# Where the queries of batch 0 are scaled, and which engine copies its first x out of PSUM, in a fused retention and feed-forward kernel

## The chip, the cores and the metric

The kernel runs on one core of one Trainium2 chip. The metric is the device time of an execution in microseconds (us): lower is better. A core has TensorE (PE, with its weight loads listed as PEld), VectorE (DVE), ScalarE (ACT), GpSimd (POOL) and SyncE (SP), which here only issues DMAs. Each engine works through its own queue in order and waits on semaphores for the others.

## The reference

Retention over 8 batches, 8 heads, 576 positions and a head dimension of 64 gives x; a feed-forward layer with a tanh gelu follows. Inputs and output are 32-bit floats, PE works in 16 bits.

```python
scale = 1.0 / np.sqrt(D_)                       # D_ = 64
scores = scale * np.matmul(q, k.transpose(0, 1, 3, 2))
gamma = 1.0 - 2.0 ** (-5.0 - np.arange(H))      # one decay per head
Dmat = np.where(rel >= 0, gamma[:, None, None] ** rel[None, :, :], 0.0)   # rel = i - j
attn = np.matmul(scores * Dmat[None], v)
x = attn.transpose(0, 2, 1, 3).reshape(B * S, H * D)                      # 4608 x 512
g = gelu_tanh(x @ w_in)                          # 512 x 2048
out = g @ w_out                                  # 2048 x 512
```

## The kernel before

**Attention of one batch.** The decay gamma^(i-j) is split into a factor of the query's position and a factor of the key's. The key's factor is put on the values when they are cast (`cast_v`, L260, values times `sc`). The query's factor, with the scale, is put on x when it leaves PSUM (`evac`, L593, times the table `gx`). Between positions i >= j inside a chunk only a mask is then left (`mask_sc`, L451: scores `st` times `cm` into `ret`).

576 positions are four chunks of 128 and a tail of 64. Two chunks are a *half* `s` (0 or 1), four heads a group `hh` (0 or 1). For each of the four (s, hh): `load_qkv` brings 256 KB of k, q or v; `cast_qk` casts k and q to 16 bits through `copy` (L247) on an engine that the plan names; `tr` (L361) transposes them on PE, and copies the result `tr` to `T` (L247); `back` (L421) transposes the keys back and copies them to `kq`; `score_mm` (L438) makes the scores `st`. For each half, `state_mm` (L506) makes the chunks' states `us` from keys and values, `scan` (L522 adds into `vs`, L526 multiplies by `gt` into `ws`) carries the state from chunk to chunk, `put` casts it into the block-diagonal buffer `tbd` (two casts of 64 partitions; with `S2` one goes to ACT and one to DVE), `values` (L553) multiplies `ret` with the values into `xs`, `inter_mm` (L580) adds the part of the earlier chunks from `tbd`, and `evac` writes x. `tbd` has two buffers, for even and odd batches, zeroed by `tbd_zero` with four memsets each (L133); `inter_tail` does the same as `evac` for the tail.

Batch 0 loads its keys and queries in a layout of its own (`R4`: four positions per partition, two heads), so that one load serves a pair of heads of both halves. A transposed pair is copied by two instructions.

**Feed-forward.** `Block.up` (L641, tile `hp`) and `up_half` (L727) multiply x with `w_in_sb` and ACT applies the gelu into `gT`; `mix_sa`, `mix_sc` and `mix_d` form sums and differences of `gT` on DVE or GpSimd for a fast product scheme; `product` (L783) multiplies them with `w_out_sb`, and `settle` adds the results up. `cast_w_in(j, i, engine)` casts a quarter of a row block of w_in. A block needs x of a whole pair of batches or of a half; the first call, `F0.up_half(0, 1)`, needs two evacuated blocks of batch 0 and w_in(0, 0 to 3).

**The order** is written out by hand. `run(units, plan)` calls units of the feed-forward in turn (units 0 to 9 are empty, 10 and 11 are the first two up_half), and after each unit the steps that the plan lists for it, in the order in which they are listed. The order of those calls is the order of each engine's queue. The letters name the engine: G is GpSimd, V is DVE, A is ACT, S2 halves between ACT and DVE.

```python
    def run(units, plan):
        for i, f in enumerate(units):
            f()
            for step in plan.get(i, ()):
                step()
```

Loads go out on SP's queue in the order in which they are written; each waits for a free buffer. `warm` (L139) and `pad` (L150) put dummy matmuls on zeros in front of PE's work, so many 128-column pieces as the table `pads` gives for a place.

Of the kernel before, what the change touches and what calls it, by code (L numbers as in the profile page):

```python
# [10 lines left out]
AF = mybir.ActivationFunctionType  # L11
ALU = mybir.AluOpType
# [7 lines left out]
def kernel(  # L20
# [53 lines left out]
    for hf in half:  # L74
        nc.gpsimd.iota(p2[hf, 0:2], pattern=[[1, 2]], base=-64, channel_multiplier=2,
                       allow_small_or_imprecise_dtypes=True)
        nc.gpsimd.iota(p2[hf, 2:3], pattern=[[0, 1]], base=-64, channel_multiplier=1,
                       allow_small_or_imprecise_dtypes=True)
    ident = const.tile([128, 128], F16, name="ident")
# [18 lines left out]
    sc = const.tile([128, 2 * H + 4], F32, name="sc")  # L98
    for hh in range(2):
        nc.vector.tensor_tensor(  # L100
            out=ex[:, 8 * hh : 8 * hh + 8].rearrange("p (r h) -> p r h", r=2),
            in0=p2[:, 0:2].unsqueeze(2).to_broadcast([128, 2, 4]),
            in1=lg[:, 4 * hh : 4 * hh + 4].unsqueeze(1).to_broadcast([128, 2, 4]),
            op=ALU.mult,
        )
# [7 lines left out]

    def mask():
        c = cm.rearrange("p r s i -> p (r s i)")
        nc.vector.tensor_tensor(out=c, in0=c, in1=p2[:, 0:1].to_broadcast([128, 256]), op=ALU.is_ge)


    gx = const.tile([128, HP, 2, 64], F32, name="gx")
    for p in range(HP):  # L120
        nc.scalar.activation(out=gx[:, p], in_=gi, func=AF.Exp, bias=lg[:, 12:13], scale=lg[:, 8 + p : 9 + p])
    nc.scalar.activation(out=sc, in_=ex, func=AF.Exp, bias=0.0, scale=-1.0)
    gt = const.tile([128, HP], F32, name="gt")
# [3 lines left out]

    R4 = {(0, "k"), (0, "q")}
# [120 lines left out]
    def cast_qk(b, s, hh, key, eng):  # L249
        t = att[b].pop((key, s, hh))  # L250
        o = att[b]["kq"][:, s, hh, "kq".index(key), :]
        if (b, key) in R4:
            copy(eng, o.rearrange("p (r h d) -> p r h d", r=4, h=2), t.rearrange("p (h r d) -> p r h d", r=4, h=2))
        else:
            copy(eng, unperm(o), perm(t))
        done(t)
# [14 lines left out]
    def cast_tail(b, key, eng):  # L271
        a = att[b]
        t = a.pop((key, "t"))
        if key != "v":
            copy(eng, a["kqt"][:, "kq".index(key), :], t[:, 0:256])
            done(t)
            return
        eng.tensor_tensor(
            out=a["vt"].rearrange("p (h d) -> p h d", d=D),
            in0=t[:, 0:256].rearrange("p (h d) -> p h d", d=D),  # L280
            in1=sc[:, 16:20].unsqueeze(2).to_broadcast([128, 4, D]),
            op=ALU.mult,
        )
        done(t)
# [307 lines left out]
    def evac(b, s, c):  # L592
        nc.vector.tensor_tensor(  # L593
            out=xb[b][:, :, 2 * s + c].rearrange("p s q i -> p q s i"),
            in0=att[b]["x", s][c].rearrange("p (q s i) -> p q s i", q=4, s=2),
            in1=gx,
            op=ALU.mult,
        )

    def inter_tail(b):  # L600
        a = att[b]
        xs = a.pop("xt")
        for u in range(2):
            for s in range(2):
# [6 lines left out]
            nc.vector.tensor_tensor(  # L611
                out=xt[:, :, b, 2 * u : 2 * u + 2, :].rearrange("p s q i -> p q s i"),
                in0=xs[u][:, 0:128].rearrange("p (q i s) -> p q s i", q=2, s=2),
                in1=gx[:, 2 * u : 2 * u + 2, :, 0:32],
                op=ALU.mult,
            )
# [274 lines left out]
    def add(plan, *entries):  # L891
# [13 lines left out]
    load_qkv(0, 1, 0, "k", None)  # L905
    load_qkv(0, 1, 0, "q", None)
    load_qkv(0, 0, 1, "k", None)
# [6 lines left out]
    load_qkv(0, 1, 0, "v", None)  # L914
    load_qkv(0, 1, 1, "v", None)
    load_w_in(0, 0, E)
# [5 lines left out]
    load_w_in(1, 0, E2)  # L922
    load_w_in(2, 2, None)
    load_qkv(1, 0, 0, "k", None)
# [24 lines left out]
    load_w_out(5, E3)  # L949
    load_w_out(7, E3)  # L950
# [3 lines left out]
    load_w_out(11, H)  # L954
# [5 lines left out]
    load_qkv(2, 1, 0, "k", None)  # L960
    load_qkv(2, 0, 0, "q", None)
    load_qkv(2, 0, 0, "k", None)
    load_qkv(2, 0, 1, "q", None)
    load_qkv(2, 1, 0, "q", None)
    load_qkv(2, 0, 0, "v", None)
    load_qkv(3, 0, 1, "k", None)
    load_qkv(2, 0, 1, "k", None)
    load_qkv(2, 0, 1, "v", None)
    load_qkv(2, 1, 1, "k", None)
    load_qkv(2, 1, 1, "v", None)  # L970
    load_qkv(3, 0, 0, "q", None)
# [3 lines left out]
    load_qkv(3, 0, 0, "k", None)  # L975
    load_qkv(3, 0, 1, "q", None)
    load_qkv(3, 0, 1, "v", None)
    load_tail(1)
    load_qkv(3, 1, 1, "k", None)
# [9 lines left out]
        ("tr", 0, 1, 0, 0): 7,  # L989
        ("tr", 0, 1, 1, 0): 0,  # L990
# [6 lines left out]
        ("bk", 0, 1, 1): 1,  # L997
        ("us", 0, 0): 2,
# [5 lines left out]
        ("tr", 0, 0, 0, 1): 9,  # L1004
# [5 lines left out]
        ("tr", 0, 1, 0, 1): 1,  # L1010
        ("in", 0, 1): 11,
# [8 lines left out]
    def turn():  # L1020
# [8 lines left out]
        (0, L(cast_qk, 0, 0, 0, "q", A)),  # L1029
        (1, L(new_x, 0)),  # L1030
        (0, L(cast_qk, 0, 0, 0, "k", V)),
        (0, L(tr, 0, 0, 0, 0, V)),
        (0, L(cast_qk, 0, 1, 0, "k", A)),
        (0, L(cast_qk, 0, 1, 0, "q", V)),
        (0, L(mask)),
        (0, L(tr, 0, 0, 0, 1, V)),
        (0, L(tr, 0, 1, 0, 0, V)),
        (2, L(score_mm, 0, 0, 0)),
        (2, L(mask_sc, 0, 0, 0)),
        (2, L(score_mm, 0, 1, 0)),  # L1040
        (2, L(back, 0, 0, 0, V)),
        (1, L(tr, 0, 1, 0, 1, S2)),
        (0, L(cast_qk, 0, 0, 1, "k", A)),
        (3, L(tr, 0, 1, 1, 1, S2)),
        (1, L(cast_qk, 0, 0, 1, "q", G)),
        (2, L(back, 0, 1, 0, A)),
        (0, L(tr, 0, 0, 1, 0, S2)),
        (1, L(cast_qk, 0, 1, 1, "q", G)),
        (5, L(back, 0, 0, 1, A)),
        (3, L(tr, 0, 0, 1, 1, A)),  # L1050
        (1, L(cast_qk, 0, 1, 1, "k", G)),
        (3, L(tr, 0, 1, 1, 0, A)),
        (5, L(mask_sc, 0, 0, 1)),
        (3, L(mask_sc, 0, 1, 0)),
        (5, L(state_mm, 0, [0])),
        (4, L(score_mm, 0, 0, 1)),
        (4, L(cast_v, 0, 0, 0, G)),
        (5, L(scan, 0, 0)),
        (5, L(values, 0, 0)),
        (6, L(score_mm, 0, 1, 1)),  # L1060
        (6, L(put, 0, 0, A)),
        (3, L(cast_v, 0, 0, 1, G)),
        (5, L(scan, 0, 1)),
        (1, L(inter_mm, 0, 0, 0)),
        (5, L(put, 0, 1, S2)),
        (7, L(back, 0, 1, 1, A)),
        (6, L(mask_sc, 0, 1, 1)),
        (8, L(inter_mm, 0, 0, 1)),
        (5, L(evac, 0, 0, 0)),
        (8, L(evac, 0, 0, 1)),  # L1070
        (9, L(inter_mm, 0, 1, 0)),
        (6, L(cast_v, 0, 1, 1, G)),
        (7, L(state_mm, 0, [1])),
        (5, L(cast_v, 0, 1, 0, G)),
        (7, L(scan, 0, 2)),
        (7, L(put, 0, 2, S2)),
        (8, L(inter_mm, 0, 1, 1)),
        (9, L(evac, 0, 1, 0)),
        (7, L(values, 0, 1)),
        (9, L(cast_w_in, 0, 2, G)),  # L1080
        (0, L(tbd_zero, 0, G)),
        (7, L(tbd_zero, 1, G)),
        (11, L(scan, 0, 3)),
        (9, L(evac, 0, 1, 1)),
        (7, L(cast_w_in, 0, 3, A)),
# [4 lines left out]
        (11, L(put, 0, 3, V)),  # L1090
        (12, L(cast_qk, 1, 0, 0, "k", G)),
        (14, L(cast_w_in, 2, 3, G)),
        (11, L(cast_qk, 1, 0, 1, "k", V)),
        (7, L(cast_w_in, 1, 3, A)),
        (10, L(cast_w_in, 2, 1, A)),
        (12, L(F0.mix_sc, 0, 2, V)),
        (8, L(cast_w_in, 1, 1, A)),
        (7, L(cast_w_in, 1, 0, V)),
        (10, L(cast_w_in, 2, 2, V)),
        (12, L(F0.mix_sa, 0, 2, V)),  # L1100
        (9, L(cast_w_in, 2, 0, V)),
        (18, L(F0.mix_d, 0, 2, V)),
        (7, L(turn)),
        (7, L(cast_w_in, 1, 2, A)),
        (19, L(F0.mix_sc, 2, 2, V)),
        (10, L(cast_qk, 1, 0, 0, "q", A)),
        (18, L(cast_qk, 1, 0, 1, "q", V)),
        (19, L(cast_w_in, 3, 0, A)),
        (19, L(tr, 1, 0, 1, 1, A)),
        (15, L(tr, 1, 0, 1, 0, S2)),  # L1110
        (15, L(tr, 1, 0, 0, 0, S2)),
        (17, L(cast_w_in, 3, 2, G)),
        (19, L(score_mm, 1, 0, 0)),
        (19, L(F0.mix_sa, 2, 2, G)),
        (22, L(mask_sc, 1, 0, 1)),
        (27, L(scan, 1, 1)),
        (29, L(inter_mm, 1, 0, 0)),
        (15, L(tr, 1, 0, 0, 1, S2)),
        (21, L(cast_v, 1, 0, 1, V)),
        (19, L(cast_w_in, 3, 1, A)),  # L1120
        (20, L(cast_v, 1, 0, 0, G)),
        (21, L(F0.mix_d, 2, 2, V)),
        (20, L(mask_sc, 1, 0, 0)),
        (21, L(new_x, 1)),
        (22, L(state_mm, 1, [0])),
        (24, L(cast_qk, 1, 1, 0, "k", G)),
        (21, L(score_mm, 1, 0, 1)),
        (14, L(cast_w_in, 3, 3, G)),
        (22, L(scan, 1, 0)),
        (22, L(put, 1, 0, A)),  # L1130
        (23, L(inter_mm, 1, 0, 1)),
        (20, L(cast_qk, 1, 1, 0, "q", A)),
        (22, L(values, 1, 0)),
        (29, L(put, 1, 1, A)),
        (27, L(F0.mix_sc, 4, 2, G)),
        (23, L(cast_qk, 1, 1, 1, "q", A)),
        (25, L(cast_v, 1, 1, 0, V)),
        (25, L(tr, 1, 1, 0, 0, V)),
        (23, L(evac, 1, 0, 1)),
        (21, L(cast_qk, 1, 1, 1, "k", A)),  # L1140
        (22, L(evac, 1, 0, 0)),
        (22, L(F0.mix_sa, 4, 2, G)),
        (27, L(cast_v, 1, 1, 1, V)),
        (24, L(tr, 1, 1, 0, 1, A)),
        (28, L(state_mm, 1, [1])),
        (28, L(F0.mix_d, 4, 2, V)),
        (27, L(tr, 1, 1, 1, 0, A)),
        (31, L(mask_sc, 1, 1, 0)),
        (28, L(score_mm, 1, 1, 0)),
        (29, L(score_mm, 1, 1, 1)),  # L1150
        (27, L(tr, 1, 1, 1, 1, A)),
        (31, L(mask_sc, 1, 1, 1)),
        (32, L(inter_mm, 1, 1, 1)),
        (29, L(scan, 1, 2)),
        (29, L(put, 1, 2, A)),
        (30, L(mix_w_out, 0, "sums", G)),
# [3 lines left out]
        (31, L(inter_mm, 1, 1, 0)),  # L1160
        (32, L(mix_w_out, 1, "sums", G)),
        (28, L(mix_w_out, 1, "copy", A)),
# [83 lines left out]
        (48, L(inter_tail, 0)),  # L1246
# [317 lines left out]
```

## Time and profile before

| | before |
|---|---|
| median of 4 runs | 298.24 us (298.08 to 298.73) |
| the profiled execution | 298.08 us, of which the span is 296.3 |
| PE busy | 290.1 us (98% of the span) |
| DVE busy | 238.6 us (81%) |
| ACT busy | 164.0 us (55%) |
| POOL busy | 98.2 us (33%) |
| first feed-forward matmul (L727) | at 22.63 us |

Times in the profile count from the start of the span. "Busy" adds up the execution of instructions on an engine, whatever they wait for elsewhere; a busy PE includes dummy matmuls. In a view with `<-` in brackets, the number is the idle time ahead of an instruction and the name is what ended it. A group's row gives the operation, output <- input with partitions x elements and type, how many there were, their busy time and the mean time of one in ns.

### The profile page before, as it was taken

What the parts mean: (1) busy time and instruction counts of PE and PEld (TensorE: products, weight loads), DVE (VectorE), ACT (ScalarE), POOL (GpSimd) and SP (SyncE); (2) the same over time, 40 slices, a digit from 0 to 9 for tenths busy, and PEclk for the clock granted to TensorE, in tenths of its full rate; (3) what the DMA queues carried; (4) which work ended last, traced back from release to release, by engine and by line L of the source; (5) the groups of instructions that cost most, each with busy time, mean ns of one, the idle gap of its engine ahead of it and who ended that gap; (6) DMA issues with size and microseconds to landing.
All of it is one profiled execution on the core that took longest, in us unless ns stands there. A gap on an engine that the chain in (4) does not pass through costs nothing.

```text
span 296.3 us, 8812 instructions
## 1 busy us (share of the span) xinstructions
PE 290.1 (98%) x3689; PEld 207.0 (70%) x3689; DVE 238.6 (81%) x456; ACT 164.0 (55%) x320; POOL 98.2 (33%) x131
## 2 busy tenths in 40 slices
PE   8989999999999999999999999999999999999995
PEld 5657478888885568655875587558754886787684
DVE  3898889989997999888569846899688198886773
ACT  7449889973736672565446544554445316605830
POOL 4572595056260336075037006698000000000000
PEclk9999999999999999999999999999999999999999
DMA  6999999767799989995996989482120002002204
GB/s 206 337 341 318 312 382 320 208 167 209 194 254 221 254 254 162 271 317 107 203 300 214 160 216 280 129 152 12 52 92 2 1 28 117 2 0 73 71 0 144
DMA packets 92663, 52.48 MB, mean 177 GB/s; under 512 B 38352, under 2 KB 86480, under 8 KB 92624
## 3 DMA queue, kind: packets, MB, share of 16 engines
q1 hardware_dynamic: 92288, 51.26, 64.4%
q10 hardware_dynamic: 336, 0.66, 0.8%
q8 instruction: 29, 0.48, 0.7%
q14 instruction: 10, 0.08, 0.1%
HBM read 36.70 MB, written 9.44 MB: 156 GB/s over the span
## 4 chain that ended last, share of the span: by engine, by line
PE 92%; ACT 4%; DVE 2%; issue 1%; DVEq 0%; ACTq 0%
PE hp L641 30%; PE my L783 11%; PE mz L783 10%; PE hp L727 6%; PE mu L783 5%; PE mv L783 5%; PE mw L783 5%; PE xs L553 3%; PE st L438 3%; PE py L671 2%; PE xs L580 2%; PE us L506 2%; PE tr L361 1%; PE warm L139 1%; PE pv L671 1%; PE tr L150 1%
## 5 line engine op out<-in xcount | busy, mean ns | idle before, releaser
L641 PE MATMUL hp<-x,w_in_sb 128*128 128x512 f16 x400 | 92.4, 379 | 0.5 <-ACT gT L645 0.2
L645 ACT ACTIVATE gT<-hp 128x512 f16<-128x512 f32 x108 | 63.8, 597 | 44.2 <-PE hp L641 43.5
L641 PEld LDWEIGHTS <-w_in_sb 128*128 128x128 f16 x432 | 40.8, 98 | 43.0 <-issue 0.7
L783 PEld LDWEIGHTS <-gT 128*128 128x128 f16 x576 | 55.8, 98 | 8.1 <-ACT gT L714 0.2
L451 DVE TENSOR_TENSOR ret<-st,cm 128x512 f16<-128x512 f32 x64 | 40.0, 680 | 4.2 <-PE st L438 4.2
L260 POOL TENSOR_TENSOR cv<-ld,sc 128x512 f16<-128x512 f32 x28 | 30.2, 1095 | 34.5 <-DMA ld<-in_v_dram 34.5
L247 POOL CAST kq<-ld 128x512 f16<-128x512 f32 x27 | 18.8, 702 | 56.5 <-DMA ld<-in_k_dram 33.9
L247 ACT CAST tbd<-ws 64x256 f16<-64x256 f32 x56 | 22.3, 402 | 22.1 <-DVE ws L526 21.6
L783 PE MATMUL my<-w_out_sb,gT 128*128 128x256 f16 x288 | 34.5, 273 | 0.0
L783 PE MATMUL mz<-w_out_sb,gT 128*128 128x256 f16 x288 | 34.4, 273 | 0.0
L783 PEld LDWEIGHTS <-gsum 128*128 128x128 f16 x288 | 28.0, 98 | 3.3
L752 DVE TENSOR_TENSOR gsum<-gT 128x1024 f16<-128x1024 f16 x35 | 28.0, 801 | 1.4 <-ACT gT L733 0.8
L756 DVE TENSOR_TENSOR gT<-gT 128x1024 f16<-128x1024 f16 x35 | 28.8, 841 | 0.2
L593 DVE TENSOR_TENSOR x<-xs,gx 128x512 f16<-128x512 f32 x32 | 21.7, 683 | 3.9 <-PE xs L580 3.7
L744 DVE TENSOR_TENSOR gdia<-gT 128x512 f16<-128x512 f16 (+1 forms) x32 | 17.0, 532 | 5.0 <-ACT gT L645 2.6
L810 DVE TENSOR_TENSOR ost<-ost,mv 128x512 f32<-128x512 f32 x18 | 11.5, 681 | 11.6 <-issue 7.5
L247 ACT CAST kq<-ld 128x512 f16<-128x512 f32 x27 | 16.4, 616 | 4.8 <-DMA ld<-in_q_dram 3.1
L727 PE MATMUL hp<-x,w_in_sb 128*128 128x256 f16 x160 | 18.8, 273 | 0.0
L783 PE MATMUL mw<-w_out_sb,gdia 128*128 128x256 f16 x144 | 17.2, 273 | 0.0
L783 PE MATMUL mu<-w_out_sb,gsum 128*128 128x256 f16 x144 | 17.2, 273 | 0.0
L783 PE MATMUL mv<-w_out_sb,gsum 128*128 128x256 f16 x144 | 17.2, 273 | 0.0
L727 PEld LDWEIGHTS <-w_in_sb 128*128 128x128 f16 x160 | 15.3, 98 | 2.2 <-issue 0.3
(119 smaller groups left out, 396.6 us busy)
## 6 DMA issues: line engine op xcount, KB each, us to landing
ld<-in_k_dram SPq DMA_DIRECT2D x30, 256.0 KB, 5.0
ld<-in_q_dram SPq DMA_DIRECT2D x30, 256.0 KB, 5.5
ld<-in_v_dram SPq DMA_DIRECT2D x30, 256.0 KB, 5.6
out_dram<-ost SPq DMA_DIRECT2D x14, 512.0 KB, 5.4
loan<-in_moe_w_out_dram SPq DMA_DIRECT2D x12, 256.0 KB, 5.8
loan<-in_moe_w_in_dram SPq DMA_DIRECT2D x8, 256.0 KB, 6.8
ld<-in_moe_w_in_dram SPq DMA_DIRECT2D x8, 256.0 KB, 5.8
ld<-in_moe_w_out_dram SPq DMA_DIRECT2D x4, 256.0 KB, 5.4
```

The lines of the kernel that those rows point to most:

```text
L247: (eng.copy if eng is nc.scalar else eng.tensor_copy)(out=out, in_=in_)
L260: eng.tensor_tensor(out=unperm(att[b]["v"][:, s, hh, :]), in0=perm(t), in1=sc[:, 8 * hh : 8 * hh + 8] .rearrange("p (r h) -> p r h", r=2) ...
L451: nc.vector.tensor_tensor(out=x.rearrange("p (a m) -> p a m", a=2), in0=st[hl].rearrange("p (a m) -> p a m", a=2), in1=cm.rearrange("p r s ...
L593: nc.vector.tensor_tensor(out=xb[b][:, :, 2 * s + c].rearrange("p s q i -> p q s i"), in0=att[b]["x", s][c].rearrange("p (q s i) -> p q s ...
L641: nc.tensor.matmul(hp, w_in_sb[:, ct, 128 * f : 128 * f + 128], x[:, :, ct, :], start=(ct == 0), stop=(ct == 3),)
L645: nc.scalar.activation(out=self.g(f // 2)[:, f % 2], in_=hp, func=AF.Gelu_apprx_tanh)
L727: nc.tensor.matmul(hp[:, 256 * h : 256 * h + 256], w_in_sb[:, ct, 256 * j + 128 * h : 256 * j + 128 * h + 128], xb[self.b][:, :, 2 * u : 2 ...
L744: e.tensor_tensor(out=self.sa[:, j : j + n], in0=g[:, :, 0, 0:256], in1=g[:, :, 1, 256:512], op=ALU.add)
L752: e.tensor_tensor(out=self.sc[:, j : j + n], in0=g[:, :, 0], in1=g[:, :, 1], op=ALU.add)
L756: e.tensor_tensor(out=g.rearrange("p j h c -> p j (h c)")[:, :, 256:768].rearrange("p j (h c) -> p j h c", h=2), in0=g[:, :, :, 0:256], in ...
L783: nc.tensor.matmul(t[u] if isinstance(t, list) else t[:, 256 * u : 256 * u + 256], lhs(j, slice(128 * u, 128 * u + 128)), w_out_sb[:, j, w ...
L810: nc.vector.tensor_tensor(out=out, in0=in0, in1=t, op=op)
```

## The change

**Queries of batch 0 are scaled at their cast** (`QS = {0}`). Two new tables hold the query's factor: `sq4` for batch 0's layout (from four new IOTAs `p4`, a product on DVE and an exp on ACT that is placed ahead of the four of `gx`) and `sq` for the tail (an exp on ACT after that of `sc`). Casting a query becomes a product with a table, and goes to DVE or GpSimd instead of ACT, DVE or GpSimd. **The four `evac` of batch 0 become copies on ACT**, where they were products on DVE; the tail's two become copies on DVE.

**Steps change place and engine.** In batch 0: the first k cast goes from DVE to GpSimd, the copy of its transpose from DVE to ACT, the last k cast (0,1,1) from GpSimd to DVE, the copy of back(0,0,0) from DVE to ACT; `tbd_zero(1)` now follows the GpSimd cast of w_in(0,2) instead of leading it. Later: the casts of w_in(1,3) and (1,1) go from ACT to GpSimd and w_in(1,2) from ACT to DVE; cast_v(1,1,0) from DVE to GpSimd; the copies of tr(1,1,0,0) from DVE to ACT and of tr(1,0,0,0) from both to DVE; put(1,1) from ACT to both. Some loads and some dummy matmuls move.

```diff
+    p4 = const.tile([128, 4], F32, name="p4")
+    for i in range(4):
+        nc.gpsimd.iota(p4[32 * i : 32 * i + 32], pattern=[[1, 4]], base=-64, channel_multiplier=4,
+                       allow_small_or_imprecise_dtypes=True)
...
+    sq4 = const.tile([128, 4, H], F32, name="sq4")
+    nc.vector.tensor_tensor(
+        out=sq4,
+        in0=p4.unsqueeze(2).to_broadcast([128, 4, H]),
+        in1=lg[:, 0:H].unsqueeze(1).to_broadcast([128, 4, H]),
+        op=ALU.mult,
+    )
...
     gx = const.tile([128, HP, 2, 64], F32, name="gx")
+    nc.scalar.activation(out=sq4, in_=sq4, func=AF.Exp, bias=lg[:, 12:13], scale=1.0)
     for p in range(HP):
         nc.scalar.activation(out=gx[:, p], in_=gi, func=AF.Exp, bias=lg[:, 12:13], scale=lg[:, 8 + p : 9 + p])
     nc.scalar.activation(out=sc, in_=ex, func=AF.Exp, bias=0.0, scale=-1.0)
+    nc.scalar.activation(out=sq, in_=ex, func=AF.Exp, bias=lg[:, 12:13], scale=1.0)
...
         if (b, key) in R4:
-            copy(eng, o.rearrange("p (r h d) -> p r h d", r=4, h=2), t.rearrange("p (h r d) -> p r h d", r=4, h=2))
+            o = o.rearrange("p (r h d) -> p r h d", r=4, h=2)
+            i = t.rearrange("p (h r d) -> p r h d", r=4, h=2)
+            if key == "q" and b in QS:
+                g = 2 * (2 * hh + s)
+                f = sq4[:, :, g : g + 2].unsqueeze(3).to_broadcast([128, 4, 2, D])
+                eng.tensor_tensor(out=o, in0=i, in1=f, op=ALU.mult)
+            else:
+                copy(eng, o, i)
...
-    def evac(b, s, c):
+    def evac(b, s, c, eng=None):
+        if b in QS:
+            copy(
+                eng,
+                xb[b][:, :, 2 * s + c].rearrange("p s q i -> p q s i"),
+                att[b]["x", s][c].rearrange("p (q s i) -> p q s i", q=4, s=2),
+            )
+            return
...
     load_qkv(0, 1, 0, "k", None)
+    load_qkv(0, 0, 1, "k", None)
     load_qkv(0, 1, 0, "q", None)
-    load_qkv(0, 0, 1, "k", None)
...
     load_qkv(0, 1, 0, "v", None)
+    load_w_in(0, 0, E)
     load_qkv(0, 1, 1, "v", None)
-    load_w_in(0, 0, E)
...
-        ("tr", 0, 1, 0, 0): 7,
-        ("tr", 0, 1, 1, 0): 0,
+        ("tr", 0, 1, 0, 0): 5,
+        ("tr", 0, 1, 1, 0): 4,
...
-        (0, L(cast_qk, 0, 0, 0, "q", A)),
+        (0, L(cast_qk, 0, 0, 0, "q", V)),
         (1, L(new_x, 0)),
-        (0, L(cast_qk, 0, 0, 0, "k", V)),
-        (0, L(tr, 0, 0, 0, 0, V)),
+        (0, L(cast_qk, 0, 0, 0, "k", G)),
+        (0, L(tr, 0, 0, 0, 0, A)),
...
-        (2, L(back, 0, 0, 0, V)),
+        (2, L(back, 0, 0, 0, A)),
...
+        (2, L(cast_qk, 0, 1, 1, "k", V)),
         (1, L(cast_qk, 0, 1, 1, "q", G)),
...
-        (1, L(cast_qk, 0, 1, 1, "k", G)),
...
+        (5, L(evac, 0, 0, 0, A)),
+        (7, L(inter_mm, 0, 0, 1)),
         (6, L(mask_sc, 0, 1, 1)),
-        (8, L(inter_mm, 0, 0, 1)),
-        (5, L(evac, 0, 0, 0)),
-        (8, L(evac, 0, 0, 1)),
+        (8, L(evac, 0, 0, 1, A)),
...
+        (7, L(cast_w_in, 0, 2, G)),
         (7, L(values, 0, 1)),
-        (9, L(cast_w_in, 0, 2, G)),
+        (9, L(evac, 0, 1, 0, A)),
+        (7, L(tbd_zero, 1, G)),
         (0, L(tbd_zero, 0, G)),
-        (7, L(tbd_zero, 1, G)),
+        (9, L(evac, 0, 1, 1, A)),
         (11, L(scan, 0, 3)),
-        (9, L(evac, 0, 1, 1)),
...
-        (7, L(cast_w_in, 1, 3, A)),
+        (9, L(cast_w_in, 1, 3, G)),
...
-        (8, L(cast_w_in, 1, 1, A)),
+        (8, L(cast_w_in, 1, 1, G)),
...
-        (7, L(cast_w_in, 1, 2, A)),
+        (8, L(cast_w_in, 1, 2, V)),
...
-        (25, L(cast_v, 1, 1, 0, V)),
-        (25, L(tr, 1, 1, 0, 0, V)),
+        (25, L(tr, 1, 1, 0, 0, A)),
+        (25, L(cast_v, 1, 1, 0, G)),
...
-        (48, L(inter_tail, 0)),
+        (48, L(inter_tail, 0, V)),
```

Of `pads`, five more places change by one or two pieces: tr(0,0,0,1) from 9 to 11, us(0,0) from 2 to 3, in(0,1) from 11 to 10, bk(0,1,1) and tr(0,1,0,1) from 1 to 0. In all two pieces of 128 columns more are multiplied, in one instruction fewer. In the loads, k(1,0,0) moves one place ahead, w_out(11) four ahead, and those of batches 2 and 3 change places among themselves by up to seven.

## The prediction

> **What bounds the kernel now.** I read the slices first, then what PE waits for, then the chain of waits where PE does wait, then the timeline of the other engines there. The page's slices (each 7.4 us):
>
> ```profile
> PE   8989999999999999999999999999999999999995
> DVE  3898889989997999888569846899688198886773
> PEclk9999999999999999999999999999999999999999
> ```
>
> TensorE works at its full clock all through; only the first three slices leave room. The view of what PE waits for between 0 and 22.6 us has four rows, two of which can be moved by this change:
>
> ```profile
> PE us L506 <- ACT kq L247: 0.6, 1, 0.6
> PE xs L553 <- DVE ret L451: 0.2, 1, 0.2
> ```
>
> (line <- what it waited for: us in all, times, longest.) The same view from 22.6 to 110 us shows one row of 0.2 us. So the 273.7 us from the first feed-forward matmul (hp L727, at 22.63) to the end of the span are matmul work, and **the time moves with the moment at which hp L727 starts**. Much of PE's work ahead of it is dummy matmuls (L139, L150), so a busy PE hides real waits there. The chain of waits shows them:
>
> ```profile
> 17.16 1.19 DVE tbd L247
> 18.35 0.03 issue
> 18.38 0.69 DVE x L593
> 19.07 1.21 DVE ret L451 x2
> 20.27 0.04 issue
> 20.32 0.41 PE xs L553 x15
> 20.73 0.70 PE us L150 x3
> ...
> 22.63 3.65 PE hp L727 x32
> ```
>
> (start, length, what.) For 3 us VectorE is the chain: half a put, an evacuation, two masked scores. Beside the chain, on DVE, stand the last scan and put of batch 0, and around them, on the timeline:
>
> ```profile
> 20.18 0.41 DVE L522 TENSOR_TENSOR vs<-us,ws 128x256 f32<-128x256 f32 x1
> 20.70 0.43 DVE L526 TENSOR_TENSOR ws<-vs,gt 128x256 f32<-128x256 f32 x1
> 21.23 0.29 DVE L247 CAST tbd<-ws 64x256 f16<-64x256 f32 x1
> 16.29 1.92 POOL L133 MEMSET tbd<- 128x512 f16 x4
> 18.30 0.59 ACT L247 COPY kq<-tr 128x512 f16<-128x512 f16 x1
> 18.93 0.32 PE L506 MATMUL us<-cv,kq 64*64 64x64 f16 x16 [0.59 <-ACT kq L247]
> 12.30 4.04 POOL L260 TENSOR_TENSOR cv<-ld,sc 128x512 f16<-128x512 f32 x4 [0.68 <-DMA ld<-in_v_dram]
> ```
>
> The same half put takes 0.29 at 21.23 and 1.19 at 17.16, and ends just after GpSimd's four memsets of the second tbd buffer: 0.90 us are a blocked DVE.
>
> **What the Trainium skill says.** "SBUF — State Buffer", section "Who interferes with whom": a DVE copy or cast in a two-port mode and a GpSimd instruction lock each other out for a whole instruction; a DVE operation with two SBUF inputs is disturbed by GpSimd reads, not by one that only writes. The trace agrees on both: the cast above (1.19 against 0.29), and a two-input scan at 16.63, under the same memsets, took its usual 0.42. "TensorE: Matmul & The Clock Gate", section "What's actually happening": the clock halves after an idle window of about 3.4 us; here the longest wait ahead of hp was 1.1 us and the clock stayed whole, so a wait that grows by tenths costs its length only.
>
> **The change, part by part.** Prices, from the groups by shape:
>
> ```profile
> L260 DVE TENSOR_TENSOR cv<-ld,sc 128x512 f16<-128x512 f32 x2 | 1.4, 691 | 0.0
> L817 ACT COPY ost<-mw 128x512 f32<-128x512 f32 x9 | 5.3, 586 | 6.0 <-PE mw L783 6.0
> L260 POOL TENSOR_TENSOR cv<-ld,sc 128x512 f16<-128x512 f32 x28 | 30.2, 1095 | 34.5 <-DMA ld<-in_v_dram 34.5
> ```
>
> (busy us, mean ns.) They stand for a scaled query cast on DVE (0.69, in place of a cast of 0.43), an evacuation as a ScalarE copy (0.59, in place of 0.68 on DVE) and a scaled query cast on GpSimd (1.10, 1.04 where it ran alone, in place of 0.61).
>
> *Set-up.* Four IOTAs on GpSimd (0.13 each, those of p2), one small DVE product (about 0.16, as ex), two more exps on ACT (0.2 busy, step 0.11, as sc and gt). sq4 is the first of ACT's exps and waits for GpSimd's four IOTAs, so gx, sc, gt, the table load and the first ACT job slip by some 0.5 us (5.39 to 5.9). Queued behind them is now the copy of the first transposed keys, which DVE started at 6.07: level to 0.1 late.
>
> *Up to 15.65.* The second half's keys load one place earlier and the first half's second query one later. Successive loads were first used at 7.42, 8.10 and 8.91, so a place is 0.7 to 0.8 us: k01, cast on ACT at 8.10, lands about 7.4; q10, cast on DVE at 7.42, lands 8.1 and costs 0.69 instead of 0.43. Both feed transposes ahead of which dummy matmuls stand: two pieces of 128 columns fewer before one, two and four more before two others; with the smaller changes two more in all, at some 0.06 us each (the chain's twelve at 20.73 took 0.70). The copy of back(0,0,0) moves from DVE to ACT, which stood idle for 2.02 us before 11.91. k11 moves from GpSimd (its second cast at 10.46 to 11.63) to DVE; q11 takes its time there as a product, so the four value casts still start when v lands (12.30). All of it ends in the scan at 15.65, with a chain of matching length: 0, between −0.3 and +0.3.
>
> *15.65 to hp.* tbd_zero(1) now comes behind the cast of w_in(0,2), whose load keeps its place (17.29), so the put at 17.16 finds GpSimd idle: −0.90. The evacuation L593 at 18.38 leaves DVE (step 0.61). The two masked scores then run from 17.75 to 19.03, not 18.99 to 20.27; their scores were complete at 17.71. ACT does the other half puts (17.15 to 17.55), then the first evacuation (0.6), w_in(0,3) (0.6) and only then the kq copy: 18.5 to 19.1 instead of 18.30 to 18.88. PE's second half of us waits for that copy and ends at 19.47, not 19.25. This is **what is late next**: the last scan, which started at 20.18 because DVE was busy, starts at 19.5 because PE delivers then. Scan 19.5 to 20.45, put (halves on ACT and DVE) to 20.9, then PE's last inter steps, which took 0.97 from 21.66 to 22.63: hp at 21.95, **−0.7**. The values need the masked scores at 19.03, so their 0.2 us goes too, inside this gap.
>
> *Can hp be ready?* It needs two evacuated x blocks and w_in(0,3), (0,2), (0,1), (0,0). On GpSimd: (0,2) 17.3 to 17.9, memsets (1.92) to 19.8, the two others (0.6 each) to 21.0. On ACT: w_in(0,3) to 18.6, the second evacuation, behind the put, to 21.5. Both within 0.5 us of the need; cover is there, not much.
>
> *After hp.* DVE loses cast_v(1,1,0) (1.41 and 1.21 of the two there were drawn out by GpSimd) and a T copy (0.42), gains one weight cast (0.43); ACT loses three weight casts and gains the T copy. GpSimd takes two weight casts (0.6 each) and cast_v (1.1) in a stretch (25 to 30 us) where it was busy for 1.46 us of 5. What can be won on PE are two gaps in the records there, 0.22 at 36.51 inside the values and 0.17 at 50.07, 0.39 together; I choose three quarters of it, **−0.3**, between −0.4 and 0 (a loss here is the first rival).
>
> *At nothing:* the loads of w_out(11) and of batches 2 and 3 that change places; SP's queue issues the same DMAs, none more, and each of 256 KB is moved past others by up to seven places of 0.8 us. The nearest use, a k cast of batch 2 on ACT, came at 68.89, when the rest of the queue was already thin (slices 10 to 16 hold 2 to 9 tenths). Batch 0's tail products on GpSimd and the two tail evacuations as DVE copies save some tenths of DVE there, beside PE.
>
> *Sum:* 0 − 0.7 − 0.3 = −1.0 on the profiled execution's own 298.08 (span 296.3 and 1.78 around it), 297.1; the median of the runs is 0.16 above that execution, so 297.2. Bounds: −0.3 − 0.9 − 0.4 = −1.6 with the kq copy not late, and 0.3 − 0.7 + 0 = −0.4.
>
> **The rivals.** *Given back between 60 and 90 us.* DVE is busy for 4.86 to 5.00 us of every 5 from 70 to 90. There a value cast shut out by GpSimd takes 1.41 instead of 0.69, a gT product 1.21 instead of 0.68. With GpSimd carrying more, two such collisions (0.7 + 0.5) take back the gain where the slack ahead of a product is 0.67: about 298.2. For it: the saturation. Against: the moved casts lie at 23 to 43 us, and an earlier hp shifts both engines alike.
>
> *The other side: k11's cast on DVE misses its gap.* It is the one cast moved into DVE's queue ahead of batch 0's masked scores, in the place of the copy of back(0,0,0) (12.00), with room only before GpSimd starts its four value casts at 12.30. q10's later load, and the dearer products, push DVE's queue; if k11 is issued after 12.30, the casts, back to back to 16.35, can hold it. Everything of the second half (its transposed keys, back(0,1,1), the scores at 17.29) is behind it. Locked out for one cast it costs about the gain; for all four it adds 4.0 less 1.0: about **301**. It decides from a delay of 0.3 us in that stage. Against it: DVE had idled 0.40 before 10.80 and 0.39 before 12.80, and one lock seldom outlasts one instruction.
>
> *It does not do what it says:* the memsets' lock leaves the put, but the kq copy behind the evacuation and w_in(0,3) on ACT slips by 0.8, or w_in(0,0) on GpSimd is late by as much: hp at 22.6, 298.1. It shares its sign and its outcome with the first rival.
>
> **How the numbers follow.** 0.2% is 0.6 us, about what a measurement of this kernel can tell from no change. Forecast (−1.0, with its bounds −1.6 to −0.4): 0.75, of which 0.02 falls within 0.2%. The first and third rival together: 0.10, about no change. The k11 rival: 0.15, half of it with one cast's lock and ending up to 1 us slower, half worse. The range goes from 296.1, half a microsecond past the better bound (296.6), to 298.6, which takes in the rivals of no change and leaves out the lock by four casts and part of that by one. Predicted 297.2 us.
>
> **What the profile after would show.** Right: the half put near 17.1 takes 0.29; no L593-type product for batch 0 on DVE; masked scores end near 19.0; hp starts at 21.9 or a little earlier; the wait of us on kq stays, at 0.6 to 0.8. Wrong: a DVE cast of kq near 12 us that takes over 1 us; PE waiting for w_in or x ahead of hp; hp on time but new PE waits between 30 and 90 us.

## The result, and the profile after

The change made the kernel slower: a median of 300.16 us (297.83 to 303.56, 43 runs) against 298.39 us (297.27 to 302.12, 64 runs) for the kernel before; the ratio is 1.0042, with a 95% interval of 1.0027 to 1.0057. The ratio leaves out executions more than 1.5% above the fastest of their kernel. The forecast was 297.2 us, with a range of 296.1 to 298.6.

Every execution also has its mean granted TensorE clock. Of 44 executions of the changed kernel, 12 had a mean clock of 0.992 to 0.994, with a median time of 302.19; the 32 others had 0.998 or more, with a median of 299.32. Of the 185 executions of the kernel before that ran beside the experiments, one had a clock below 0.997. So there are two losses: about 0.9 us at full clock (299.32 against 298.39), and some 3 us more in a quarter of the executions. I call an execution of a clock below 0.997 *clocked down* in what follows.

The profiled execution of the changed kernel is one of its best: 298.40 us, span 296.4, full clock. It shows how the forecast gain failed to come, but not the whole loss. Of the 0.32 us by which it is above the profiled execution before, 0.19 lie outside the span: the time of an execution exceeds the span by 1.81 us on average in the 185 executions of the kernel before and by 1.99 in the 44 of the changed kernel. The forecast had taken over the old 1.78. The versions of the changed kernel below have 1.9 to 2.1, while g1, e2 and f2, made from the kernel before, have 1.8; what takes this time the profiles don't show.

The page's slices:

```profile
PE   8989999999999999999999999999999999999995
DVE  3896979989997987898569746899688198886774
PEclk9999999999999999999999999999999999999999
```

What PE waited for between 0 and 110 us (line <- what it waited for: us in all, times, longest):

```profile
PE xs L606 <- DVE tbd L263: 1.1, 1, 1.1
...
PE xs L579 <- DVE ret L477: 0.4, 1, 0.4
...
PE tr L387 <- DVE kq L263: 0.2, 1, 0.2
```

The wait of us for the kq copy is gone from the list, and a longer one for a put has come in its place. On the timeline (start, length, engine, line, what; in brackets the idle time before and what ended it):

```profile
11.87 4.23 POOL L286 TENSOR_TENSOR cv<-ld,sc 128x512 f16<-128x512 f32 x4 [0.74 <-DMA ld<-in_v_dram]
12.24 0.95 DVE L263 CAST kq<-ld 128x512 f16<-128x512 f32 x1
16.04 0.60 POOL L263 CAST w_in_sb<-loan 128x512 f16<-128x512 f32 x1
16.59 1.91 POOL L149 MEMSET tbd<- 128x512 f16 x4
17.67 0.98 DVE L263 CAST tbd<-ws 64x256 f16<-64x256 f32 x1
21.01 0.69 DVE L263 CAST tbd<-ws 64x256 f16<-64x256 f32 x1
21.84 0.38 PE L606 MATMUL xs<-T,tbd 128*128 128x128 f16 x4 [1.14 <-DVE tbd L263]
22.61 3.66 PE L760 MATMUL hp<-x,w_in_sb 128*128 128x256 f16 x32
```

The first feed-forward matmul starts at 22.61, where it started at 22.63; 21.95 was forecast. The keys' cast on DVE met the value casts (0.95 us where 0.43 is usual), and the scan that the forecast left at 15.65 started at 16.15. GpSimd took the cast of w_in(0,2) at 16.04, not at 17.3, so the memsets ran to 18.50 and the half put at 17.67 was held all the same: 0.98 us, not 0.29. The second put took 0.69 beside GpSimd's next cast. From hp to the end it is 273.82 us, against 273.67 before.

### The profile page after: what moved, and what is told of

Same layout as the page of the kernel before. It is cut to its first block, busy times and chain, and to the rows that moved or that the text cites. A ratio compares the mean times of both kernels' runs of the same rounds, so it can differ in the third digit from the quotient of the medians.

```text
span 296.4 us, 8818 instructions
## 1 busy us (share of the span) xinstructions
PE 289.4 (98%) x3688; PEld 206.8 (70%) x3688; DVE 234.4 (79%) x451; ACT 165.2 (56%) x324; POOL 103.8 (35%) x138
## 4 chain that ended last, share of the span: by engine, by line
PE 87%; DVE 7%; ACT 4%; issue 1%; DVEq 0%
PE hp L674 27%; PE mz L816 10%; PE my L816 10%; PE hp L760 6%; PE mu L816 5%; PE mv L816 5%; PE mw L816 5%; PE xs L579 3%; PE py L704 2%; PE st L464 2%; PE xs L606 2%; PE us L532 1%; PE tr L387 1%; DVE ret L477 1%; PE warm L155 1%; PE pv L704 1%
## 5 line engine op out<-in xcount | busy, mean ns | idle before, releaser
L286 POOL TENSOR_TENSOR cv<-ld,sc 128x512 f16<-128x512 f32 x28 | 32.1, 1164 | 32.9 <-PE tr L387 12.9
L263 POOL CAST kq<-ld 128x512 f16<-128x512 f32 x25 | 17.4, 700 | 52.1 <-DMA ld<-in_k_dram 44.9
L789 DVE TENSOR_TENSOR gT<-gT 128x1024 f16<-128x1024 f16 x35 | 27.2, 795 | 0.3
L626 DVE TENSOR_TENSOR x<-xs,gx 128x512 f16<-128x512 f32 x28 | 18.9, 681 | 5.5 <-PE xs L606 5.4
L777 DVE TENSOR_TENSOR gdia<-gT 128x512 f16<-128x512 f16 (+1 forms) x32 | 18.0, 562 | 5.3 <-ACT gT L678 2.9
L263 ACT CAST kq<-ld 128x512 f16<-128x512 f32 x26 | 15.7, 618 | 5.1 <-DMA ld<-in_q_dram 3.9
```

The costliest lines, as they stand in the source:

```text
L263: (eng.copy if eng is nc.scalar else eng.tensor_copy)(out=out, in_=in_)
L286: eng.tensor_tensor(out=unperm(att[b]["v"][:, s, hh, :]), in0=perm(t), in1=sc[:, 8 * hh : 8 * hh + 8] .rearrange("p (r h) -> p r h", r=2) ...
L626: nc.vector.tensor_tensor(out=xb[b][:, :, 2 * s + c].rearrange("p s q i -> p q s i"), in0=att[b]["x", s][c].rearrange("p (q s i) -> p q s ...
L777: e.tensor_tensor(out=self.sa[:, j : j + n], in0=g[:, :, 0, 0:256], in1=g[:, :, 1, 256:512], op=ALU.add)
L789: e.tensor_tensor(out=g.rearrange("p j h c -> p j (h c)")[:, :, 256:768].rearrange("p j (h c) -> p j h c", h=2), in0=g[:, :, :, 0:256], in ...
```

## The experiments

Each profile is one execution, so profiles show mechanisms and the ratios show sizes. All of these are against the kernel before, run on the same chip. The profiles of g1, e1, f1, e3 and g2 are of clocked-down executions: there the clock is at half for one stretch of 3.41 us that starts between 21.4 and 25.1 us, which makes most of these starts of hp later too.

| kernel | median us | ratio (95%) | clocked down | first hp us |
|---|---|---|---|---|
| after | 300.16 | 1.0042 (1.0027 to 1.0057) | 12 of 44 | 22.61 |
| g1_before_memset_behind | 299.34 | 1.0031 (1.0012 to 1.0049) | 6 of 19 | 23.77 |
| f2_before_new_loads | 299.03 | 1.0023 (1.0003 to 1.0042) | 2 of 22 | 22.27 |
| e2_before_k11_dve | 298.80 | 1.0015 (1.0001 to 1.0028) | 0 of 22 | 22.02 |
| e1_k11_gpsimd | 299.30 | 1.0033 (1.0013 to 1.0052) | 2 of 22 | 23.58 |
| e4_memsets_early | 299.09 | 1.0025 (1.0009 to 1.0040) | 2 of 22 | 22.32 |
| f1_old_loads | 298.49 | 1.0026 (1.0003 to 1.0048) | 5 of 14 | 23.36 |
| f3_inter_back | 299.71 | 1.0050 (1.0031 to 1.0069) | 2 of 22 | 22.20 |
| f4_four_undone | 297.91 | 0.9991 (0.9978 to 1.0004) | 0 of 22 | 21.82 |
| g3_kq_first | 297.71 | 0.9985 (0.9966 to 1.0004) | 1 of 14 | 21.57 |
| g2_batch0_only | 299.34 | 1.0039 (1.0021 to 1.0057) | 2 of 21 | 24.35 |
| g5_undone_unscaled | 299.94 | 1.0063 (1.0039 to 1.0087) | 0 of 7 | 23.96 |
| e3_unscaled | 302.36 | 1.0135 (1.0110 to 1.0160) | 5 of 5 | 23.57 |

**The memsets behind the cast of w_in(0,2), alone in the kernel before** (g1_before_memset_behind).

```diff
-        (9, L(cast_w_in, 0, 2, G)),
+        (7, L(cast_w_in, 0, 2, G)),
+        (7, L(tbd_zero, 1, G)),
         (0, L(tbd_zero, 0, G)),
-        (7, L(tbd_zero, 1, G)),
```

> The kernel before with the memsets of the second tbd buffer behind GpSimd's cast of w_in(0,2), nothing else. Theory M (w_in(0,2) has mostly landed when GpSimd is done with its value casts, so the memsets only start 0.6 us later, at some 16.6 to 17.0, and the half put on DVE is held to their end): that put ends at 18.5 to 19.1 instead of 18.35, the first feed-forward matmul comes 0.2 to 0.6 later, ratio 1.001. The forecast (w_in(0,2) lands at 17.29, the put goes ahead of the memsets in 0.29 us): 0.5 to 0.9 us earlier, ratio 0.998.

Its timeline:

```profile
16.10 0.61 POOL L247 CAST w_in_sb<-loan 128x512 f16<-128x512 f32 x1
16.65 1.93 POOL L133 MEMSET tbd<- 128x512 f16 x4
17.09 1.62 DVE L247 CAST tbd<-ws 64x256 f16<-64x256 f32 x1
23.77 1.45 PE L727 MATMUL hp<-x,w_in_sb 128*128 128x256 f16 x7
```

The put is held to 18.71, later than the 18.35 of the kernel before, and the ratio is 1.0031, more than theory M gave it. This step was the chief term of the forecast gain; alone, it costs 0.31% (0.12 to 0.49). Theory M holds, and the other profiles bear it out. Six of them are of kernels with the memsets behind this cast: the put took 1.62 in four, 0.98 in the changed kernel, and 0.29 in one alone (f3 below). In the four with the old order and the put on DVE it took 1.19, 1.16, 0.75 and 0.43. So the 0.90 us that were to be won were themselves one of the larger draws.

**The same memsets in GpSimd's idle stretch, in the changed kernel** (e4_memsets_early).

```diff
-        (7, L(tbd_zero, 1, G)),
         (0, L(tbd_zero, 0, G)),
+        (0, L(tbd_zero, 1, G)),
```

> The changed kernel with the four memsets of the second tbd buffer put right behind those of the first, into GpSimd's idle stretch from 6.1 to 8.6 us. Theory L: the half put at 17.67 no longer meets them (0.98 us there, 0.29 without a lock), unless the cast of w_in(0,1) on GpSimd takes their place; the first feed-forward matmul comes 0.3 to 0.7 earlier, ratio 1.001 to 1.003. Rival S: PE waits for the states and not for this put, ratio 1.004.

The put took 0.52 (at 17.38) beside the casts of w_in, hp came at 22.32, and the ratio is 1.0025: as theory L has it, though its interval (to 1.0040) just takes in the rival's 1.004 and overlaps that of the changed kernel. This profile also showed something that I had not looked for, at 88 us:

```profile
84.06 2.40 POOL L286 TENSOR_TENSOR cv<-ld,sc 128x512 f16<-128x512 f32 x2 [4.79 <-DMA ld<-in_v_dram]
88.43 0.40 PE L606 MATMUL xs<-T,tbd 128*128 128x128 f16 x4 [1.29 <-POOL tbd L263]
```

GpSimd waited for values of batch 3, and the put of chunk (2,2) stands behind them in its queue; PE waited 1.29 us for it. In the profile of the kernel before those value casts started at 81.94, and PE did not wait.

**The order of the loads of batches 2 and 3**, undone in the changed kernel (f1_old_loads) and put alone into the kernel before (f2_before_new_loads). The edit exchanges the lines of the loads behind `load_w_out(5, E3)` for those of the other kernel:

```diff
-    load_w_out(11, H)
     load_w_out(7, E3)
...
-    load_qkv(2, 1, 1, "k", None)
     load_qkv(3, 0, 1, "q", None)
```

> The changed kernel with the order of the loads behind w_out(5), batches 2 and 3 and w_out(11), as it was before; all else as changed. Theory P (the put of chunk (2,2) on GpSimd comes late at 85 to 89 us, because the value casts of batch 3 ahead of it in its queue wait for later loads; 1.29 and 1.70 us of PE's wait in two of the runs above): that wait is gone in the profile, fewer executions at full clock lie above 299.5, ratio to before falls by 0.002, to about 1.002. Rival H (these loads are hidden, and the loss lies ahead of the first feed-forward matmul): ratio unchanged at 1.004.

> The kernel before with only the new order of the loads behind w_out(5). Theory P: PE waits for the put of (2,2) in a part of the executions, up to 1.3 us; ratio 1.001 to 1.004. Rival H: 1.000.

At full clock the median falls from 299.32 to 298.26 with the old order, and 8 of those 9 executions are below 298.6, where 26 of the changed kernel's 32 were at 298.6 or above. Alone in the kernel before, the new order costs 0.23% (1.0003 to 1.0042), with a full-clock median of 298.97 against 298.25. So the size is shown. Theory P is not: neither of the two profiles has the wait at 88 us. Of the six profiles with the new order two have it (e3 with 1.7 us, e4); of the kernel before and the seven other kernels of the table with the old order, one (g5 below, 1.1 us). That is too few to tell the orders apart. The ratio of f1 is no better than 1.0026 because 5 of its 14 executions were clocked down.

**The PE step inter_mm(0,0,1) with its dummy matmuls, back behind the values** (f3_inter_back).

```diff
-        (7, L(inter_mm, 0, 0, 1)),
         (6, L(mask_sc, 0, 1, 1)),
+        (8, L(inter_mm, 0, 0, 1)),
```

> The changed kernel with the step inter_mm(0,0,1), and the dummy matmuls that stand with it, back behind the values of the second half, where they were. Theory C (these ten pieces used to cover PE's wait for the last put; bare, the 1.1 to 1.3 us let the clock gate take the clock down for some 3.4 us in a part of the executions, a quarter of them in the changed kernel): no execution below a mean clock of 0.997, the PE wait of L606 for tbd falls from 1.1 to under 0.6, the median falls by 0.5 us or more, ratio 1.002. Rival: the clock loss comes from the start of the kernel, and stays in a quarter of the executions.

Why it was tried: in the windows of f1_old_loads (stretch, then its length, busy time of PE, PEld, DVE, ACT and POOL, PE's clock, DMA share, GB/s) the clock falls right where PE waits for the put:

```profile
20.00:22.60 2.60, 1.00 (x20) 0.71 (x20) 2.36 (x6) 0.89 (x2) 1.98 (x3) 0.91 1.07 335
22.60:26.00 3.40, 3.40 (x21) 2.55 (x20) 2.11 (x7) 1.67 (x3) 0.63 (x1) 0.56 1.15 327
```

With the dummy matmuls back in that gap, the wait fell to 0.50, and 2 of 22 executions were clocked down instead of 12 of 44. That goes the way of theory C, which expected none, but it does not show it: such a difference can be chance (p = 0.12 in an exact test), and e1 and e4, which leave these pieces where the change put them, had 2 of 22 each as well. The rest of theory C failed: the full-clock median stayed (299.51 against 299.32) and the ratio did not fall. Nor is the bare place the whole cause of the clock's fall: g1 lost its clock in the old PE order, with several shorter waits. The profile of f3 is also the one in which w_in(0,2) landed late, as the forecast had it:

```profile
17.04 0.29 DVE L263 CAST tbd<-ws 64x256 f16<-64x256 f32 x1
17.36 0.61 POOL L263 CAST w_in_sb<-loan 128x512 f16<-128x512 f32 x1 [1.17 <-DMA loan<-in_moe_w_in_dram]
17.91 1.92 POOL L149 MEMSET tbd<- 128x512 f16 x4
```

GpSimd stood waiting, the put went through in 0.29, and the masked scores ended at 18.92 (19.03 was forecast).

**The keys (0,1,1), cast on DVE or on GpSimd** (e1_k11_gpsimd undoes it, e2_before_k11_dve does it alone).

```diff
-        (2, L(cast_qk, 0, 1, 1, "k", V)),
+        (2, L(cast_qk, 0, 1, 1, "k", G)),
```

> The changed kernel with one letter undone: the cast of the last keys of batch 0 (0,1,1) runs on GpSimd again, behind its two query products, instead of on DVE. Theory L (locks): this cast on DVE started at 12.24 under GpSimd's value casts (from 11.87), took 0.95 us instead of 0.43, and in other executions may be held by more of them; without it the first us matmul (L532) comes at about 14.6 instead of 15.12, the first feed-forward matmul at 22.3 instead of 22.77, and the long executions (300 to 303 us) become rare: ratio to before 1.000 to 1.002. Rival S (the scaled casts and the later set-up themselves cost the time): the cast on GpSimd comes to 11.1 to 11.7 and delays the value casts to match, ratio unchanged at 1.004.

> The kernel before with this cast alone moved: the keys of (0,1,1) are cast on DVE behind the first masked scores, nothing else. Theory L: the cast takes 0.9 us or more under the value casts, the executions spread to 300 and above as those of the changed kernel do, ratio 1.003 to 1.006. Rival S: DVE has 0.4 us idle there on either side, GpSimd is relieved of 0.6, ratio 0.999 to 1.001.

In e2 the cast took 0.70 (at 12.12, under value casts from 11.50); the ratio is 1.0015, below what theory L gave and above the rival's. In e1 the first us came earlier (14.49 instead of 15.05), but hp did not (23.58, clocked down from 22.12): the put was held for 1.62 by the memsets, and the ratio of 1.0033 is above the 1.000 to 1.002 of theory L and cannot be told from the changed kernel's. So this rival of the forecast was there, with one cast's lock and not four, and it is the smallest of the three losses. It does not come each time: in e3, e4, f1 and f3, which keep this cast on DVE, it took 0.42, from 11.81 to 11.90, ahead of the value casts.

**All four undone, the rest of the change kept** (f4_four_undone: the edits of e1, e4, f1 and f3 together).

> The changed kernel with four things undone or moved at once: keys (0,1,1) cast on GpSimd, memsets of the second tbd buffer in GpSimd's idle stretch, inter_mm(0,0,1) back behind the values, old order of the loads behind w_out(5). The scaled query casts, the copies of x on ScalarE and the other moves stay. If these four are the whole loss and the rest brings what was forecast (0.7 to 1.0 us): ratio 0.997 to 0.999. If the scaled casts and the later set-up cost something of their own: 1.000 to 1.002.

```profile
17.25 0.29 DVE L263 CAST tbd<-ws 64x256 f16<-64x256 f32 x1
19.17 0.32 PE L532 MATMUL us<-cv,kq 64*64 64x64 f16 x16 [1.03 <-ACT kq L263]
21.82 2.34 PE L760 MATMUL hp<-x,w_in_sb 128*128 128x256 f16 x20
```

No execution was clocked down, the put is free, and hp starts at 21.82, 0.81 us before that of the kernel before. At 34 us the lead is 0.81, at 57 us 0.63, at the end of the span 0.47, and 0.3 more goes outside the span (2.11 us there, 1.81 before). The median is 0.34 below that of the kernel before in the same set (298.25); the ratio of 0.9991 does not exclude no gain.

**The kq copy ahead of the evacuation and of w_in(0,3) on ACT** (g3_kq_first, from f4).

```diff
-        (5, L(evac, 0, 0, 0, A)),
+        (7, L(evac, 0, 0, 0, A)),
+        (7, L(cast_w_in, 0, 3, A)),
...
-        (6, L(cast_w_in, 0, 3, A)),
```

> The kernel with four things undone, and ACT's copy of kq for back(0,1,1) put ahead of the first evacuation and of the cast of w_in(0,3), behind which it stood. PE waited 1.03 us for that copy in the profile of the kernel with four things undone. If that wait sets the start of the feed-forward part: it falls to about 0.4, the first feed-forward matmul comes 0.4 to 0.6 earlier (21.3), ratio 0.997 to 0.998. Rival: the evacuation then frees its PSUM bank too late for the values, and nothing is won, ratio 0.999.

```profile
18.92 0.32 PE L532 MATMUL us<-cv,kq 64*64 64x64 f16 x16 [0.48 <-ACT kq L263]
21.57 2.67 PE L760 MATMUL hp<-x,w_in_sb 128*128 128x256 f16 x23
```

The wait falls from 1.03 to 0.48 and hp comes 0.25 earlier. This is the best version: 297.71 against 298.38 in its set, 0.9985 (0.9966 to 1.0004). It beats the changed kernel; that it beats the kernel before is likely, not shown. From hp to the end its profile takes 273.69 us, as before (273.67), where that of f4 takes 274.00.

**The later moves put back too** (g2_batch0_only: f4 with the plan from the end of batch 0 to the first tail as before).

> The kernel with four things undone (keys (0,1,1) on GpSimd, memsets early, inter_mm(0,0,1) behind the values, old loads), and with the steps of the plan from the end of batch 0 to the first tail also as before: what stays of the change is batch 0. The kernel with four things undone had its first feed-forward matmul 0.81 us earlier than before in the profile, but ended only 0.47 earlier. Theory D (the moved steps of batches 1 and 2 give 0.3 back, at the values of batch 1 and between 56 and 86 us): ratio 0.998. Rival (they bring their share, 0.3): ratio 1.000 to 1.001.

This could not answer its question. The casts of w_in(1,1), (1,2) and (1,3) came back to ACT, ahead of batch 0's evacuations there, and hp had to wait 2.37 us for x (start 24.35). What it does show is that, in this order of steps, those casts have to leave ACT once ACT evacuates x. Why f4 loses 0.34 us of its lead later stays open; as the profile of g3 loses next to nothing, it need not lie in the moved steps.

**The scaling put back** (e3_unscaled from the changed kernel, g5_undone_unscaled from f4).

```diff
-    QS = {0}
+    QS = set()
```

> The changed kernel with the scaling of batch 0 put back to where it was: its queries are cast without a factor on the same engines, its x leaves PSUM as products on DVE; every other step keeps its changed place. Theory L: the locks stay, and DVE gets 0.6 us per evacuation back, ratio 1.003 to 1.007. Rival S: without the dearer casts the ratio falls to 1.001 or below.

> The kernel with four things undone, and the scaling of batch 0 back at its evacuation on DVE, its queries cast without a factor. If taking the evacuation off DVE is worth the 0.6 us that it was given: the first feed-forward matmul comes 0.4 to 0.7 later than with it (21.82), ratio 1.001. Rival: the cheaper casts and the earlier table load make up for it, ratio 0.999.

Both are slower than with scaling, by far. e3 was clocked down in all five executions, with PE waiting for puts, masked scores and evacuations one after another. g5 mixes in a lock of its own making: its first query is a plain cast on DVE under eight memsets. The first two lines are from its timeline, the third, a product in the same place under the same memsets, from that of f4:

```profile
4.13 3.79 POOL L149 MEMSET tbd<- 128x512 f16 x8
4.32 3.88 DVE L263 CAST kq<-ld 128x512 f16<-128x512 f32 x1 [1.79 <-DMA ld<-in_q_dram]
```

```profile
4.36 0.69 DVE L274 TENSOR_TENSOR kq<-ld,sq 128x512 f16<-128x512 f32 x1 [1.84 <-DMA ld<-in_q_dram]
```

**A cleaner pair for the scaling, and the put's lock alone.** These four kernels share a base in which the DMA transposes of batches 3 to 7 are done on PE; that makes each some 12 us slower after 85 us, so their starts are compared with one another. The second differs from the first by `QS = set()` and the first query's cast on ACT; the fourth from the third by one letter:

```diff
-        (5, L(put, 0, 1, S2)),
+        (5, L(put, 0, 1, A)),
```

> The kernel with four things undone and the kq copy first, in which the transposes of batches 3 to 7, done by DMA so far, are done on PE with copies on ACT and DVE. This base is the same in all four kernels of this set and makes each of them slower from some 90 us on; what is compared is one with another. Expected: the first feed-forward matmul at 21.4 to 21.9 in the profile, as without it (21.57).

> The same, with the scaling of batch 0 back at its evacuation on DVE; its queries are cast without a factor, the first of them on ACT as in the kernel before, where GpSimd's memsets can't hold it. If taking the evacuation off DVE is worth something of its own: the first feed-forward matmul comes 0.3 to 0.7 later than in the scaled one, ratio to before higher by 0.001 to 0.002. Rival (the scaling is neutral, the gain came from the places of the memsets and of the kq copy): both within 0.2 us and 0.0005.

> The kernel before with the transposes of batches 3 to 7 on PE: the base for the next one, and for the first one of this set, which should be faster than it by 0.4 to 0.9 us if the gain of the kernel with four things undone and the kq copy first is real. First feed-forward matmul at 22.0 to 22.7.

> The kernel before with the transposes of batches 3 to 7 on PE, and both halves of the put of chunk (0,1) on ACT: GpSimd's memsets then hold no DVE instruction there. The forecast's step taken alone (0.90 us of lock, less what ACT's longer queue delays the kq copy, 0.4): the masked scores end 0.9 to 1.2 us earlier, the wait of us for kq grows from 0.59 to 1.0, the first feed-forward matmul comes 0.4 to 0.6 earlier than without. Rival (PE is held by the kq copy alone, so that it only gets worse): 0.1 to 0.4 later.

Medians: 310.62 (6 runs), 313.13 (5), 311.27 (6), 312.39 (6). First hp in the profiles of the first two:

```profile
21.28 3.65 PE L742 MATMUL hp<-x,w_in_sb 128*128 128x256 f16 x32
```

```profile
22.99 3.65 PE L742 MATMUL hp<-x,w_in_sb 128*128 128x256 f16 x32 [0.32 <-DVE x L608]
```

The scaled one is 1.7 us earlier at hp and 2.5 us faster, more than expected. Its scores at 10.26 came at 10.80 in the other, so 0.5 is won before the evacuations (the first query off ACT); the rest lies at the puts and evacuations, where DVE is the chain. Within this order of steps, which was laid out for it, the scaling is thus worth more than the 0.6 us that the forecast gave it. The first is also 0.65 us faster than the third, whose steps are in the order of the kernel before; 0.4 to 0.9 were expected. That is a second sign, from six executions each, that the gain of g3 is real.

In the other pair hp came at 22.30 with the put on ACT against 22.64, of which 0.12 was there at the scores of 13.4 us; the wait of us for kq grew to 1.11 as expected. So the lock's removal alone is worth some 0.2 us at hp, less than the 0.4 to 0.6 expected: the kq copy is next, and the lock of this base was 0.46 (the put took 0.75), not 0.90. The total went the other way, 1.1 us longer: in the profiles 0.86 us more passes between hp and the end. Why was not settled, so the totals show no gain from this step.

## Why the prediction was wrong, point by point

**The step that failed first: "tbd_zero(1) now comes behind the cast of w_in(0,2), whose load keeps its place (17.29), so the put at 17.16 finds GpSimd idle: −0.90."** The 17.29 was the landing in one execution. By the DMA records of the traces, the loads from 9 to 19 us land 0.6 to 0.9 us apart, with one pause of 1.0 to 2.2 us near 16 us: in the kernel before from 15.32 to 17.29, in the changed one from 15.54 to 17.36. In the former w_in(0,2) fell behind the pause, in the latter ahead of it, as in most profiles here: in the five other profiles with the kernel before's order of these loads it landed between 15.19 and 15.95. Then GpSimd can cast w_in(0,2) as soon as its value casts end, and "behind the cast" only moves the memsets 0.6 us further into the put. Instead of falling from 1.19 to 0.29, the put took 0.98 in the changed kernel and 1.62 in g1, which alone measured +0.31%. The working after it held where the lock was gone: scores to 18.90, last scan at 19.53 and hp at 21.82 in f4, against 19.03, 19.5 and 21.95.

**"At nothing: the loads".** They cost 0.23% when put alone into the kernel before. I named a k cast at 68.89 as the nearest use and did not follow GpSimd's queue to the value casts of batch 3 and the put behind them. That is one way in which they can cost time; that it is the way stays open.

**"A wait that grows by tenths costs its length only"** was wrong: 12 of 44 executions lost the clock, at some 3 us each. The dummy pieces that had covered the last put (eleven, now ten) went ahead with inter_mm(0,0,1), and I took PE's order for unchanged. In the five profiles whose clock fell, PE's longest wait ahead of the fall was 0.7 to 2.4 us. With all four steps undone (f4) none of 22 executions was clocked down; which of them keeps the clock is not shown.

**The k11 rival** came true in its mild form: 0.95 us where 0.43 is usual, 0.15% alone. Here too one trace was one draw: the value casts mostly start when their load lands, which gave 12.30 in the trace that I had and gives 11.48 to 12.40 in all of them; the new order of the first loads does not move this load. In the profile after, this took 0.5 us of the "0, between −0.3 and +0.3" up to the scan at 15.65; in e3, e4, f1 and f3 that scan is at 15.51 to 15.60. The argument against this rival, "one lock seldom outlasts one instruction", did not fit the forecast's own lines: the put at 17.16 had been held for 0.90 us by memsets that take 0.48 each. The changed kernel did end on this rival's side, but its main cause was not in it.

**After hp, −0.3** did not come: from hp to the end it is 273.67 us before, 273.82 in the changed kernel, 273.69 in g3 and 274.00 in f4. And the 1.78 us around the span became 1.97.

**Right:** hp's start is what counts; the kq copy is late next (1.03 in f4); the evacuation off DVE is a gain. The three single measurements add up to 0.69% (0.31, 0.23, 0.15), and f4 puts the rest at −0.09%: together 0.60%, just above the measured 0.27 to 0.57%. They need not add up, since the locks and the clock act on the same waits. (The price of a dummy piece holds, though the 0.70 us at 20.73 are eleven pieces, not twelve.)

## What to carry to other kernels

When a step is moved to avoid a collision on a shared port, ask what decides its start: if that is a DMA's landing, one trace gives one draw of it, and the move is safe only if it holds for an early and a late landing. Follow a reordered load through the whole queue of the engine that consumes it, to the last instruction behind it for which TensorE waits. Dummy matmuls belong to the wait that they cover: when their step moves, count the wait that they leave bare.

## What the runs showed of the hardware that I had not expected

- A DVE cast that meets a chain of GpSimd memsets is held to the end of the chain: 3.88 us under eight, 1.62 under a rest of four. Meeting GpSimd products it got in after one: 0.95 at 12.24, while they ran on to 16.10. The Trainium skill ("SBUF — State Buffer", section "Who interferes with whom") gives the lock for a whole instruction; that a chain of memsets holds it throughout is what these runs add.
- The Trainium skill ("TensorE: Matmul & The Clock Gate", section "What's actually happening") has the clock halve after an idle window of about 3.4 us. Here it fell although PE was never idle for that long: in f1_old_loads its longest wait was 1.54 us, and it was busy for 1.65 of the 3.41 us ahead of the fall. In all five profiles whose clock fell, PE was busy for 1.04 to 2.04 us of the 3.41 ahead of it, and the clock was at half for 3.41 us. In the 13 that kept it, the least busy stretch of 3.41 us between 9 and 26 us held at least 1.97 us of work; the changed kernel's, with a wait of 1.14, held 2.23. So a thinly filled stretch goes with the fall, not one long wait; as the two groups overlap (2.04 fell, 1.97 did not), these profiles give no limit.
